# Chunk 10's gate and value weights: the low half made by an adding transfer from GpSimd's queue

## The chip, the cores and the metric

The program runs on one core of a Trainium2 chip. The metric is the device time of one execution in microseconds (us). The engines are TensorE (PE, with its weight loads shown apart as PEld), VectorE (DVE), ScalarE (ACT), GpSimd (POOL) and SyncE (SP), which issues the kernel's transfers.

## The reference, cut to what matters

Attention with a window of 16 and block summaries gives x, 3072 tokens by 512. A gated feed-forward layer follows:

```
def _moe_ref(x, w_gate, w_val, w_out):
    g = x @ w_gate                        # 512 -> 1536
    silu = g * (1.0 / (1.0 + np.exp(-g)))
    val = x @ w_val                       # 512 -> 1536
    return (silu * val @ w_out).astype(np.float32)
```

The weights come as 64-bit floats, and the answer must be exact enough that one reduced-precision product of TensorE does not do.

## The kernel before, in words

The feed-forward width of 1536 is cut into twelve chunks of 128, and the tokens into six blocks of 512. For each block and chunk TensorE computes `gate(k,j)` (12 matmuls of 128x512), `val(k,j)` (12 more) and later `down(k,j)` (12 more, into four accumulators). Twelve, because each of the four 128-row pieces of the contraction takes three products: every operand is split into a high part, rounded to TensorE's fast 32-bit format (fp32r), and a low part, the rest. The order of the three in a gate is `(wl, xh)`, `(wh, xl)`, `(wh, xh)`, so the first matmul of a gate reads the low half of the weights.

The weights are read once, while the first block (k = 0) and the second block's attention are computed. Each chunk's weights go through these steps, which the kernel names in a list written out by hand (`PROLOGUE`): `w_load` (SP, the raw 64-bit words), `w_abs` (ACT), `w_c1`, `w_c2`, `w_s1`, `w_s2` (DVE, which put the 32-bit float together bit by bit into the tile `m`), `w_hi` (a rounding copy of `m` into the high half, `=a` on ACT) and `w_lo` (`m` minus the high half into the low half, `=d` on DVE or `=p` on POOL). `gv` stands for gate and value together (128x1024), `o` for the output weights (128x512). Both halves of a chunk lie in one tile, `w_gv10` for chunk 10.

Every engine executes its instructions in the order of that list. Around the place of the change DVE does `w_lo(10,gv)`, then `w_c1(8,o)`, `w_c2(9,o)` and the key maxima of `keys(1,3)` (line 336), which overwrite a buffer that POOL's copy `kw` of the same step reads first. POOL does `w_lo(6,o)` and then the two `kw` copies of `keys(1,3)`. TensorE does `gate(0,8) val(0,8) down(0,6) tr0(1,2)`, a small transpose `pv` and then `gate(0,10)`, the first reader of `w_gv10`. After `room(1)` the memory of the tiles `m` of the chunks up to 10 is given to chunk 11's weights: SP loads `raw_v`, `raw_g` and `raw_o` of chunk 11 there.

Of the kernel before, what the change touches and what calls it, by code (L numbers as in the profile page):

```python
# [10 lines left out]
F32 = mybir.dt.float32  # L11
F32R = mybir.dt.float32r
I32 = mybir.dt.int32
AF = mybir.ActivationFunctionType
ALU = mybir.AluOpType
# [3 lines left out]
DM = H * D  # L19
DFF = 1536  # L20
BLK, WIN = 32, 16
P = 128
# [110 lines left out]
exp0(1,2) w_lo(8,gv)=d exp1(1,2) down(0,5) ah(0,7)=d w_c1(9,o) w_s2(7,o) w_c1(6,o) w_hi(7,o)=a al(0,7)=d  # L133
split(1,1)=a w_lo(9,gv)=p w_lo(7,o)=d w_c2(10,gv) w_c2(6,o) ah(0,6)=a w_abs(8,o) w_s1(10,gv) gate(0,9) w_s1(6,o)
val(0,9) down(0,7) w_s2(10,gv) silu(0,9) al(0,6)=d w_s2(6,o) gate(0,8) rcp(1,2) w_hi(6,o)=a mul(0,9) w_lo(6,o)=p
pool_values(1,2) w_hi(10,gv)=a load(1,3) w_lo(10,gv)=d w_c1(8,o) silu(0,8) w_c2(9,o) val(0,8) nrm(1,2)=a
keys(1,3) w_abs(10,o) down(0,6) tr0(1,2) load_values(1,2) rest(1,1) room(1) w_load(11,v) ah(0,9)=a w_s1(9,o)
w_c2(8,o) w_s1(8,o) mul(0,8) w_s2(8,o) values(1,2)=a w_load(11,g) pt0(1,2)=d w_s2(9,o) w_hi(8,o)=a gate(0,10)
ah(0,8)=a w_hi(9,o)=a tr1(1,2) w_lo(9,o)=p w_lo(8,o)=d al(0,9)=d pt1(1,2)=a w_load(11,o) silu(0,10) scores(1,3)
w_abs(11,v) out(1,2) w_abs(11,g) down(0,9) ttr0(1,3) ttr1(1,3) exp0(1,3) w_c1(11,g) al(0,8)=p load_values(1,3)  # L140
w_c1(11,v) w_c2(11,g) w_c1(10,o) w_s1(11,g) w_c2(10,o) w_s2(11,g) w_c2(11,v) exp1(1,3) w_hi(11,g)=a w_s1(10,o)
w_s1(11,v) val(0,10) w_s2(11,v) rcp(1,3) w_s2(10,o) w_lo(11,g)=d down(0,8) gate(0,11) mul(0,10) w_hi(10,o)=a
w_abs(11,o) nrm(1,3)=a tr0(1,3) pool_values(1,3) w_c1(11,o) w_c2(11,o) w_hi(11,v)=d w_lo(11,v)=d split(1,2)=d
w_lo(10,o)=d silu(0,11) w_s1(11,o) val(0,11) ah(0,10)=d rest(1,2) al(0,10)=d tr1(1,3) pt0(1,3)=a mul(0,11)
w_s2(11,o) values(1,3)=a w_hi(11,o)=d down(0,10) pt1(1,3)=d ah(0,11)=a al(0,11)=d out(1,3) split(1,3)=a
w_lo(11,o)=p rest(1,3) down(0,11) load(2,0)
"""


# [8 lines left out]
def body(ctx, tc, qP, kP, vT, vP, kq, kF, qF, vE, vR, vO, wgv, wends, wo, cst_in, bias_in, out):  # L158
    nc = tc.nc
# [17 lines left out]
    def subtract(e, out, a, b):  # L177
        (nc.vector if e == "d" else nc.gpsimd).tensor_tensor(out=out, in0=a, in1=b.bitcast(F32), op=ALU.subtract)  # L178

    def copy(e, out, in_):  # L180
        if e == "a":
            nc.scalar.copy(out, in_)  # L182
        else:
            (nc.vector if e == "d" else nc.gpsimd).tensor_copy(out, in_)


    W = {}
    on = ""

    def w_pool(j):  # L190
        return wts[0 if j < NJ // 2 else 1 if j < NJ - 1 else 2]

    def w_lead(j, nm):
        return LEAD if (nm, j) == ("v", NJ - 1) else 0

    def w_load(j, nm):

        n = len(nm) * DM
        w = w_pool(j).tile([P, w_lead(j, nm) + 2 * n], I32, tag=f"{nm}{j}", name=f"raw_{nm}{j}")[:, w_lead(j, nm) :]
        src = wo[j] if nm == "o" else wgv[j] if nm == "gv" else wends[j > 0, "gv".index(nm)]  # L200
        nc.sync.dma_start(w, src.bitcast(I32))  # L201
        W[nm, j] = w.rearrange("p (n t) -> p n t", t=2)

    def w_abs(j, nm):
        low, high = (W[nm, j][:, :, t] for t in range(2))
        if nm != "o" and j < NJ - 1:
            m = dec.tile([P, len(nm) * DM], F32, tag="m", name=f"m_{nm}{j}")
        else:
            m = mlp.tile([P, DM], F32, tag="o", bufs=3, name=f"m_{nm}{j}")
        nc.scalar.activation(out=m, in_=high.bitcast(F32), func=AF.Abs)  # L210
        W[nm, j] = low, high, m
# [19 lines left out]
    def w_rest(j, nm):  # L231
# [3 lines left out]
            out=f, in0=low, scalar=29, in1=f, op0=ALU.logical_shift_right, op1=ALU.bitwise_or  # L235
        )

    def w_hi(j, nm):
        m = W[nm, j][2]
        n = w_lead(j, nm) + 2 * len(nm) * DM  # L240
        w = w_pool(j).tile([P, n], F32R, tag=f"{nm}{j}", name=f"w_{nm}{j}")
        w = w[:, w_lead(j, nm) :].rearrange("p (t n d) -> p t n d", t=2, d=DM)
        hi, lo = (w[:, t].rearrange("p n d -> p (n d)") for t in range(2))
        copy(on or "a", hi, m)
        W[nm, j] = w, hi, lo, m

    def w_lo(j, nm):
        w, hi, lo, m = W[nm, j]
        subtract(on or "d", lo, m, hi)
        for i, x in enumerate(nm):  # L250
            W[x, j] = (w[:, 0, i], w[:, 1, i])


    KT, VT, ksum, vsum, X, U = {}, {}, {}, {}, {}, {}
# [570 lines left out]
    for n in WARM:  # L825
# [8 lines left out]
        "rcp": a_inverse, "nrm": a_scale, "tr0": lambda k, u: a_turn(k, u, 0), "tr1": lambda k, u: a_turn(k, u, 1),  # L834
        "pt0": lambda k, u: a_turned(k, u, 0), "pt1": lambda k, u: a_turned(k, u, 1),
        "out": a_out, "outp": a_out_pooled, "split": a_split, "rest": a_rest, "w_load": w_load, "w_abs": w_abs, "w_c1": w_range,
        "w_c2": w_shift, "w_s1": w_top, "w_s2": w_rest, "w_hi": w_hi, "w_lo": w_lo, "gate": m_up_gate,
        "silu": m_silu, "val": m_up_val, "mul": m_mul, "ah": m_high, "al": m_low, "down": m_down,
        "values": a_values, "load_values": a_load_values, "keys": a_keys, "pool_values": a_pool_values,
        "exp": a_exp, "norm": a_norm,  # L840
# [6 lines left out]
    on = ""  # L847
# [101 lines left out]
```

## Time and profile before

| what | value |
|---|---|
| timed runs, median (lowest to highest) | 674.22 us (673.66 to 674.47) |
| profiled execution, span from first to last instruction | 672.2 us |
| PE busy | 665.8 us, 99% of the span |
| DVE, ACT, POOL busy | 340.3, 292.8 and 140.9 us |
| transfers from SP's queue | 59.39 MB |

The profile lists no time of its own for the profiled execution beside its span. The median of the timed runs is 2.0 us above that span, so a span is turned into a time by adding 2.0 us. Times inside the trace count from the start of the span.

### The profile page before, as it was taken

Reading aid. Unit: us, or ns where it says so; the run is one execution under the profiler, and the core shown is the slowest. Engines: PE = TensorE matmul, PEld = TensorE weight load, DVE = VectorE, ACT = ScalarE, POOL = GpSimd, SP = SyncE. Lnnn points to the kernel's source line nnn. Section 1 sums busy time; section 2 is a strip of 40 time slices with the busy share of each in tenths; the row PEclk is TensorE's granted clock in tenths of the full one; section 3 lists DMA queues with packets and bytes.
Section 4 is the critical chain, followed back from the end, with each engine's and each line's share of the span. In section 5 each row is a group of like instructions: output and inputs, shape, how many; then the busy total and the mean of one; then the engine's idle time right before and its main releaser. Section 6 shows DMA issues by size and latency. Waiting matters only on the chain.

```text
span 672.2 us, 12396 instructions
## 1 busy us (share of the span) xinstructions
PE 665.8 (99%) x4934; PEld 543.9 (81%) x4934; DVE 340.3 (51%) x956; ACT 292.8 (44%) x723; POOL 140.9 (21%) x137
## 2 busy tenths in 40 slices
PE   8999999999999999999999999999999999999998
PEld 6688888887888888888888888888888888888886
DVE  6999999946524526446347356363352451100002
ACT  6969897834441433424415424235254151211112
POOL 4110211123221212212112122122222221111110
PEclk9999999999999999999999999999999999999999
DMA  8979743144220223403405213012122000100001
GB/s 332 393 241 359 263 141 106 61 126 129 57 57 1 57 49 119 104 5 77 105 0 168 59 47 81 23 34 71 49 57 58 0 25 0 63 1 0 1 0 64
DMA packets 72059, 60.18 MB, mean 90 GB/s; under 512 B 42273, under 2 KB 60065, under 8 KB 70465
## 3 DMA queue, kind: packets, MB, share of 16 engines
q1 hardware_dynamic: 72000, 59.39, 28.8%
q8 instruction: 39, 0.64, 0.4%
q14 instruction: 20, 0.16, 0.1%
HBM read 53.08 MB, written 6.29 MB: 88 GB/s over the span
## 4 chain that ended last, share of the span: by engine, by line
PE 96%; DMA 2%; SPq 1%; issue 0%; ACT 0%; DVE 0%; ACTq 0%
PE g L650 30%; PE v L650 29%; PE acc L697 29%; PE xo L615 4%; DMA vrows<-in_vE 2%; PE sc L447 2%; PE pp L566 1%; PE sc L458 1%; PE xo L623 1%; PE pv L415 0%; PE end L697 0%; SPq L201 0%; SPq L290 0%; SPq L285 0%; SPq L797 0%
## 5 line engine op out<-in xcount | busy, mean ns | idle before, releaser
L697 PE MATMUL acc<-w_o,ah 128*128 128x512 f32 x572 | 176.2, 389 | 0.0
L650 PE MATMUL g<-xh,w_gv 128*128 128x512 f32 x480 | 159.3, 393 | 0.0
L650 PE MATMUL v<-xh,w_gv 128*128 128x512 f32 x480 | 158.0, 390 | 0.2 <-ACT a L656 0.2
L661 DVE TENSOR_TENSOR a<-v,a 128x512 f32<-128x512 f32 x72 | 49.6, 689 | 199.8 <-PE v L650 198.1
L178 POOL TENSOR_TENSOR al<-a,ah 128x512 fp32r<-128x512 f32 x61 | 78.6, 1288 | 312.6 <-ACT ah L182 312.6
L697 PEld LDWEIGHTS acc<-w_o,ah 128*128 128x128 f32 x572 | 107.4, 188 | 22.2
L182 ACT CAST ah<-a 128x512 fp32r<-128x512 f32 x70 | 43.4, 620 | 163.3 <-DVE a L661 163.2
L697 PE MATMUL acc<-w_o,al 128*128 128x512 f32 x286 | 111.7, 391 | 0.0
L650 PEld LDWEIGHTS g<-xh,w_gv 128*128 128x128 f32 x480 | 90.1, 188 | 20.3 <-POOL w_gv L178 0.2
L650 PEld LDWEIGHTS v<-xh,w_gv 128*128 128x128 f32 x480 | 90.1, 188 | 19.2 <-ACT a L656 0.5
L656 ACT ACTIVATE a<-g 128x512 f32<-128x512 f32 x72 | 43.0, 598 | 139.6 <-PE g L650 137.8
L596 DVE STREAM_TRANSPOSE pt_short<-p_short 32x256 f32<-32x256 f32 x192 | 83.7, 436 | 19.7 <-POOL p_short L551 16.9
L650 PE MATMUL g<-xl,w_gv 128*128 128x512 f32 x240 | 93.5, 390 | 0.0
L650 PE MATMUL v<-xl,w_gv 128*128 128x512 f32 x240 | 93.4, 389 | 0.0
L697 PEld LDWEIGHTS acc<-w_o,al 128*128 128x128 f32 x286 | 53.7, 188 | 11.4 <-DVE al L178 0.2
L650 PEld LDWEIGHTS v<-xl,w_gv 128*128 128x128 f32 x240 | 45.1, 188 | 9.2
L650 PEld LDWEIGHTS g<-xl,w_gv 128*128 128x128 f32 x240 | 45.1, 188 | 8.9
L178 DVE TENSOR_TENSOR xl<-xo,xh 128x512 fp32r<-128x512 f32 x24 | 16.4, 689 | 58.3 <-ACT xh L182 58.3
L524 ACT ACTIVATE p_short<-p_short,nm 128x88 f32<-128x88 f32 x128 | 45.3, 355 | 0.2
L551 POOL TENSOR_TENSOR p_short<-p_short,ri 128x704 f32<-128x704 f32 x16 | 25.9, 1621 | 53.9 <-DVE ri L542 49.6
L650 PE MATMUL g<-xh,w_g 128*128 128x512 f32 x96 | 32.1, 396 | 0.0
L650 PE MATMUL v<-xh,w_v 128*128 128x512 f32 x96 | 31.6, 390 | 0.0
(125 smaller groups left out, 699.6 us busy)
## 6 DMA issues: line engine op xcount, KB each, us to landing
raw_gv<-in_wgv SPq DMA_DIRECT2D x10, 1024.0 KB, 11.5
raw_o<-in_wo SPq DMA_DIRECT2D x12, 512.0 KB, 12.3
out<-o SPq DMA_DIRECT2D x23, 256.0 KB, 2.1
kt<-in_kP SPq DMA_DIRECT2D x12, 384.0 KB, 4.4
vt<-in_vT SPq DMA_DIRECT2D x12, 384.0 KB, 4.1
vw<-in_vP SPq DMA_DIRECT2D x12, 384.0 KB, 3.8
kw<-in_kP SPq DMA_DIRECT2D x12, 272.0 KB, 4.9
vw<-in_vP SPq DMA_DIRECT2D x16, 192.0 KB, 3.8
```

Source lines behind the costliest of these rows:

```text
L178: (nc.vector if e == "d" else nc.gpsimd).tensor_tensor(out=out, in0=a, in1=b.bitcast(F32), op=ALU.subtract)
L182: nc.scalar.copy(out, in_)
L447: nc.tensor.matmul(sc[h][s * SQ : (s + 1) * SQ, c * SC : (c + 1) * SC], t["q"][hs, i * SQ : (i + 1) * SQ], keys[hs], start=True, stop=True,)
L458: nc.tensor.matmul(sc[h][s * QT : (s + 1) * QT, c * KC : (c + 1) * KC], t["q"][hs, qs], t["kw"][hs, i, :], start=True, stop=True,)
L524: nc.scalar.activation(out=t["p"][:, i, :kc], in_=t["p"][:, i, :kc], func=AF.Exp, scale=-1.0, bias=t["nm"][:, i : i + 1], accum_out=t["sm" ...
L551: (nc.vector if on == "d" else nc.gpsimd).tensor_tensor(out=p, in0=p, in1=ri.rearrange("p (n o) -> p n o", o=1).broadcast_to([P, 2 * NTP, ...
L596: nc.vector.transpose(out=to[r * SQ : (r + 1) * SQ, :, s * SQ : (s + 1) * SQ], in_=t["p"][s * SQ : (s + 1) * SQ, :, at : at + SQ],)
L615: nc.tensor.matmul(ps[hs, qs], vw, t["pt"][:n, h, qs], start=k not in OWN or i == 0, stop=k not in OWN)
L650: nc.tensor.matmul(ps, w[:, cs], x, start=u == 0 and n == 0, stop=u == NP - 1 and n == 2)
L656: nc.scalar.activation(out=a, in_=A.pop(("g", k, j)), func=AF.Silu)
L661: nc.vector.tensor_tensor(out=a, in0=ps, in1=a, op=ALU.mult)
L697: nc.tensor.matmul(out, a[:, ts], w[:, cs], start=begin and n == 0, stop=end and n == 2)
```

## The change

In the list one step, `w_lo(10,gv)=d`, becomes two, `w_neg(10,gv)=d w_add(10,gv)`; every other step stands where it stood. `w_neg` writes minus `m`, rounded to fp32r, into the low half, which is minus the high half; `w_add` is a transfer inside SBUF, issued from POOL's queue, that adds `m` onto it.

```
-pool_values(1,2) w_hi(10,gv)=a load(1,3) w_lo(10,gv)=d w_c1(8,o) silu(0,8) w_c2(9,o) val(0,8) nrm(1,2)=a
+pool_values(1,2) w_hi(10,gv)=a load(1,3) w_neg(10,gv)=d w_add(10,gv) w_c1(8,o) silu(0,8) w_c2(9,o) val(0,8)
...
+    def w_parts(j, nm):
+        if len(W[nm, j]) == 3:
+            m = W[nm, j][2]
+            n = w_lead(j, nm) + 2 * len(nm) * DM
+            w = w_pool(j).tile([P, n], F32R, tag=f"{nm}{j}", name=f"w_{nm}{j}")
+            w = w[:, w_lead(j, nm) :].rearrange("p (t n d) -> p t n d", t=2, d=DM)
+            hi, lo = (w[:, t].rearrange("p n d -> p (n d)") for t in range(2))
+            W[nm, j] = w, hi, lo, m
+        return W[nm, j]
...
     def w_hi(j, nm):
...
+        w, hi, lo, m = w_parts(j, nm)
         copy(on or "a", hi, m)
...
+    def w_minus(j, nm):
+        w, hi, lo, m = w_parts(j, nm)
+        if on == "d":
+            nc.vector.tensor_scalar(out=lo, in0=m, scalar1=-1.0, scalar2=None, op0=ALU.mult)
+        else:
+            nc.scalar.activation(out=lo, in_=m, func=AF.Copy, scale=-1.0)
+
+    def w_plus(j, nm):
+        w, hi, lo, m = W[nm, j]
+        nc.gpsimd.dma_start(lo.bitcast(F32), m, accum_op=ALU.add)
+        w_ready(j, nm)
...
-        "w_c2": w_shift, "w_s1": w_top, "w_s2": w_rest, "w_hi": w_hi, "w_lo": w_lo, "gate": m_up_gate,
+        "w_c2": w_shift, "w_s1": w_top, "w_s2": w_rest, "w_hi": w_hi, "w_lo": w_lo, "w_neg": w_minus, "w_add": w_plus, "gate": m_up_gate,
```

The lines of the program below the new functions stand 21 lines further down in the changed kernel (336 becomes 357, 650 becomes 671).

The first place is where the low half is made. POOL's queue there, before and then of the changed kernel (the last number of a name is a buffer's; the brackets name the semaphores that a row waits for: an engine's, a load's from SP as DMAHW, and a POOL transfer's as DMASW):

```order
L178 TENSOR_TENSOR w_gv9_1313<-m_gv9_1022,w_gv9_1313 128x1024 [waits DMAHW0_49,Activation_49]
L178 TENSOR_TENSOR w_o6_1445<-m_o6_1085,w_o6_1445 128x512 [waits DMAHW5_49,Activation_49]
L184 COPY kw_1_3_1458<-ks_3_319 128x4x24 [waits DMAHW0_49,DMAHW1_49,PE_49,Pool_49]
L184 COPY kw_1_3_1458<-ks_3_1490 128x4x24 [waits DVE_49]
L178 TENSOR_TENSOR w_o9_1556<-m_o9_1276,w_o9_1556 128x512 [waits DMAHW4_49,DMAHW2_49,Activation_49]
```

```order
L178 TENSOR_TENSOR w_gv9_1313<-m_gv9_1022,w_gv9_1313 128x1024 [waits DMAHW0_49,Activation_49]
L178 TENSOR_TENSOR w_o6_1445<-m_o6_1085,w_o6_1445 128x512 [waits DMAHW5_49,Activation_49]
L271 DMA w_gv10_1451<-m_gv10_1332 128x1024 [waits DMAHW6_49,DMAHW2_49,DVE_49]
L184 COPY kw_1_3_1458<-ks_3_319 128x4x24 [waits DMAHW0_49,DMAHW1_49,PE_49,Pool_49]
L184 COPY kw_1_3_1458<-ks_3_1491 128x4x24 [waits DVE_49]
```

The transfer stands behind `w_lo(6,o)` and ahead of both `kw` copies, and it waits for DVE. DVE's queue at the same place, before and then of the changed kernel:

```order
L356 TENSOR_REDUCE vr_1_2_1449<-vt_1_2_1169 128x24 [waits DMAHW2_49]
L178 TENSOR_TENSOR w_gv10_1451<-m_gv10_1332,w_gv10_1451 128x1024 [waits Activation_49]
L215 TENSOR_SCALAR m_o8_1382<-m_o8_1382 128x512
L219 TENSOR_SCALAR m_o9_1276<-m_o9_1276 128x512
L336 TENSOR_REDUCE ks_3_1490<-kt_1_3_1453 128x24 [waits DMAHW7_49,Pool_49]
```

```order
L377 TENSOR_REDUCE vr_1_2_1449<-vt_1_2_1169 128x24 [waits DMAHW2_49]
L265 TENSOR_SCALAR w_gv10_1451<-m_gv10_1332 128x1024
L215 TENSOR_SCALAR m_o8_1382<-m_o8_1382 128x512
L219 TENSOR_SCALAR m_o9_1276<-m_o9_1276 128x512
L357 TENSOR_REDUCE ks_3_1491<-kt_1_3_1453 128x24 [waits DMAHW7_49,Pool_49]
```

A subtraction that waited for ACT's `w_hi` became a multiplication by -1 that waits for no other engine; the key maxima keep their wait for POOL's first `kw` copy, which now stands behind the transfer.

The second place is the first reader, TensorE's `gate(0,10)`, before and then of the changed kernel:

```order
L566 MATMUL pp0_1_2_1507<-consts_104,p_1_2_1305 120x128 [waits Activation_49] x4
L394 MATMUL pv_1_2_1530<-consts_104,vr_1_2_1449 24x128 [waits DVE_49,PE_49]
L650 MATMUL g_0_10_1541<-xh_0_0_530,w_gv10_1451 128x512
L650 MATMUL g_0_10_1541<-xl_0_0_531,w_gv10_1451 128x512
L650 MATMUL g_0_10_1541<-xh_0_0_530,w_gv10_1451 128x512
```

```order
L587 MATMUL pp0_1_2_1508<-consts_104,p_1_2_1305 120x128 [waits Activation_49] x4
L415 MATMUL pv_1_2_1531<-consts_104,vr_1_2_1449 24x128 [waits DVE_49,PE_49]
L671 MATMUL g_0_10_1542<-xh_0_0_530,w_gv10_1451 128x512 [waits DMASW0_49]
L671 MATMUL g_0_10_1542<-xl_0_0_531,w_gv10_1451 128x512
L671 MATMUL g_0_10_1542<-xh_0_0_530,w_gv10_1451 128x512
```

The order is the same, and the gate's first matmul gains a wait for the transfer. SP's queue for chunk 11's loads, before and then of the changed kernel:

```order
L329 DMA vw_1_2_1512<-in_vP 96x4x128 [waits DMAHW6_49]
L201 DMA raw_v11_1520<-in_wends 128x1024 [waits DMAHW7_49,Pool_49]
L201 DMA raw_g11_1534<-in_wends 128x1024 [waits DMAHW0_49,Activation_49]
L201 DMA raw_o11_1568<-in_wo 128x1024 [waits DMAHW1_49,DVE_49]
L329 DMA vw_1_3_1642<-in_vP 96x4x128 [waits DMAHW5_49,DMAHW2_49,DMAHW6_49,PE_49,Activation_49]
```

```order
L350 DMA vw_1_2_1513<-in_vP 96x4x128 [waits DMAHW6_49]
L201 DMA raw_v11_1521<-in_wends 128x1024 [waits DMAHW7_49,Pool_49]
L201 DMA raw_g11_1535<-in_wends 128x1024 [waits DMAHW0_49,Activation_49]
L201 DMA raw_o11_1569<-in_wo 128x1024 [waits DMASW0_49,DMAHW1_49,DVE_49,Activation_49]
L350 DMA vw_1_3_1643<-in_vP 96x4x128 [waits DMAHW5_49,DMAHW2_49,DMAHW6_49,PE_49,Activation_49]
```

Only the third of these loads, `raw_o11`, gains a wait for the transfer, because it overwrites the tile `m_gv10` that the transfer reads.

## Rows read from the trace of the kernel before

**Rows 1.** Page, part 1: each engine's busy time, share, instructions.

```profile
PE 665.8 (99%) x4934; PEld 543.9 (81%) x4934; DVE 340.3 (51%) x956; ACT 292.8 (44%) x723; POOL 140.9 (21%) x137
```

**Rows 2.** Page, part 4: the chain that ended last, by engine.

```profile
PE 96%; DMA 2%; SPq 1%; issue 0%; ACT 0%; DVE 0%; ACTq 0%
```

**Rows 3.** Waits of PE: us in total, times, longest; all others are earlier loads.

```profile
PE pv L415 <- DMA vrows<-in_vE: 1.0, 1, 1.0
...
PE v L650 <- ACT a L656: 0.2, 1, 0.2
```

**Rows 4.** Timeline of DVE, 110 to 121 us: start, duration, engine, line, operation.

```profile
110.75 1.45 DVE L178 TENSOR_TENSOR w_gv<-m_gv,w_gv 128x1024 fp32r<-128x1024 f32 x1
112.12 0.48 DVE L215 TENSOR_SCALAR m_o<-m_o 128x512 f32<-128x512 f32 x1
112.52 0.41 DVE L219 TENSOR_SCALAR m_o<-m_o 128x512 int32<-128x512 int32 x1
112.86 0.94 DVE L336 TENSOR_REDUCE ks<-kt 128x24 f32<-128x768 f32 x1
...
120.92 0.28 DVE L508 CUSTOM_DVE_ANT_0 p<-sc,bias 128x120 f32<-128x120 f32 x1 [1.25 <-PE sc L458]
```

**Rows 5.** Timeline of PEld, the weight load that opens gate(0,10).

```profile
116.42 0.19 PEld L650 LDWEIGHTS g<-xh,w_gv 128*128 128x128 f32 x1
```

**Rows 6.** Tile m_gv, one group: duration ns min/median/max, first and last start.

```profile
L215 DVE TENSOR_SCALAR m_gv<-m_gv x10: 680/686/695, 20.4 to 99.3; 128x1024 f32<-128x1024 f32 x10
```

**Rows 7.** Timeline of POOL, 109 to 114 us.

```profile
109.82 1.29 POOL L178 TENSOR_TENSOR w_o<-m_o,w_o 128x512 fp32r<-128x512 f32 x1 [10.96 <-ACT w_o L182]
111.06 1.26 POOL L184 COPY kw<-ks 128x96 f32<-128x96 f32 x1
113.86 0.27 POOL L184 COPY kw<-ks 128x96 f32<-128x96 f32 x1 [1.54 <-DMA vt<-in_vT]
```

**Rows 8.** Timeline of SP, 110 to 114 us: the loads it issues.

```profile
110.86 0.34 SPq L322 DMA_DIRECT2D vt<-in_vT  x1
111.68 0.86 SPq L329 DMA_DIRECT2D vw<-in_vP  x2
112.64 0.42 SPq L201 DMA_DIRECT2D raw_v<-in_wends  x1
113.15 0.38 SPq L201 DMA_DIRECT2D raw_g<-in_wends  x1
113.63 0.38 SPq L201 DMA_DIRECT2D raw_o<-in_wo  x1
```

**Rows 9.** Transfers issued from 100 to 135 us: count, KB each, us to landing.

```profile
raw_v<-in_wends SPq DMA_DIRECT2D x1, 512.0 KB, 5.5
raw_g<-in_wends SPq DMA_DIRECT2D x1, 512.0 KB, 6.5
raw_o<-in_wo SPq DMA_DIRECT2D x1, 512.0 KB, 7.4
vt<-in_vT SPq DMA_DIRECT2D x1, 384.0 KB, 3.2
```

**Rows 10.** Windows: length, engines busy, granted PE clock, DMA share, GB/s.

```profile
108.00:112.00 4.00, 4.00 (x19) 3.30 (x19) 3.97 (x7) 2.78 (x6) 2.18 (x2) 1.00 0.05 5
112.00:114.00 2.00, 2.00 (x11) 1.65 (x10) 2.00 (x5) 2.00 (x7) 0.46 (x2) 1.00 0.88 279
114.00:116.00 2.00, 2.00 (x11) 1.60 (x10) 1.97 (x5) 1.36 (x3) 0.13 (x1) 1.00 0.95 280
116.00:118.00 2.00, 2.00 (x13) 1.73 (x12) 2.00 (x5) 1.16 (x3) 0.00 (x0) 1.00 1.01 384
```

**Rows 11.** Timeline of ACT: the first reader of chunk 11's raw_o.

```profile
129.30 0.67 ACT L210 ACTIVATE m_o<-raw_o 128x512 f32<-128x512 f32 x1
```

**Rows 12.** Page, part 6: a load of twice the size, median us to landing.

```profile
raw_gv<-in_wgv SPq DMA_DIRECT2D x10, 1024.0 KB, 11.5
```

**Rows 13.** The chain that ended last: twelve matmuls of a gate.

```profile
107.98 2.72 PE g L650 x12
```

More of the change, by code (lines that the diff above doesn't have):

```diff
@@ L135 @@
 val(0,9) down(0,7) w_s2(10,gv) silu(0,9) al(0,6)=d w_s2(6,o) gate(0,8) rcp(1,2) w_hi(6,o)=a mul(0,9) w_lo(6,o)=p
-pool_values(1,2) w_hi(10,gv)=a load(1,3) w_lo(10,gv)=d w_c1(8,o) silu(0,8) w_c2(9,o) val(0,8) nrm(1,2)=a
-keys(1,3) w_abs(10,o) down(0,6) tr0(1,2) load_values(1,2) rest(1,1) room(1) w_load(11,v) ah(0,9)=a w_s1(9,o)
-w_c2(8,o) w_s1(8,o) mul(0,8) w_s2(8,o) values(1,2)=a w_load(11,g) pt0(1,2)=d w_s2(9,o) w_hi(8,o)=a gate(0,10)
-ah(0,8)=a w_hi(9,o)=a tr1(1,2) w_lo(9,o)=p w_lo(8,o)=d al(0,9)=d pt1(1,2)=a w_load(11,o) silu(0,10) scores(1,3)
@@ L140 @@
[L140 to L144, printed above, removed]
@@ L145 @@
-w_s2(11,o) values(1,3)=a w_hi(11,o)=d down(0,10) pt1(1,3)=d ah(0,11)=a al(0,11)=d out(1,3) split(1,3)=a
-w_lo(11,o)=p rest(1,3) down(0,11) load(2,0)
+pool_values(1,2) w_hi(10,gv)=a load(1,3) w_neg(10,gv)=d w_add(10,gv) w_c1(8,o) silu(0,8) w_c2(9,o) val(0,8)
+nrm(1,2)=a keys(1,3) w_abs(10,o) down(0,6) tr0(1,2) load_values(1,2) rest(1,1) room(1) w_load(11,v) ah(0,9)=a
+w_s1(9,o) w_c2(8,o) w_s1(8,o) mul(0,8) w_s2(8,o) values(1,2)=a w_load(11,g) pt0(1,2)=d w_s2(9,o) w_hi(8,o)=a
+gate(0,10) ah(0,8)=a w_hi(9,o)=a tr1(1,2) w_lo(9,o)=p w_lo(8,o)=d al(0,9)=d pt1(1,2)=a w_load(11,o) silu(0,10)
@@ new lines @@
+scores(1,3) w_abs(11,v) out(1,2) w_abs(11,g) down(0,9) ttr0(1,3) ttr1(1,3) exp0(1,3) w_c1(11,g) al(0,8)=p
+load_values(1,3) w_c1(11,v) w_c2(11,g) w_c1(10,o) w_s1(11,g) w_c2(10,o) w_s2(11,g) w_c2(11,v) exp1(1,3)
+w_hi(11,g)=a w_s1(10,o) w_s1(11,v) val(0,10) w_s2(11,v) rcp(1,3) w_s2(10,o) w_lo(11,g)=d down(0,8) gate(0,11)
+mul(0,10) w_hi(10,o)=a w_abs(11,o) nrm(1,3)=a tr0(1,3) pool_values(1,3) w_c1(11,o) w_c2(11,o) w_hi(11,v)=d
+w_lo(11,v)=d split(1,2)=d w_lo(10,o)=d silu(0,11) w_s1(11,o) val(0,11) ah(0,10)=d rest(1,2) al(0,10)=d tr1(1,3)
@@ L147 @@
+pt0(1,3)=a mul(0,11) w_s2(11,o) values(1,3)=a w_hi(11,o)=d down(0,10) pt1(1,3)=d ah(0,11)=a al(0,11)=d out(1,3)
+split(1,3)=a w_lo(11,o)=p rest(1,3) down(0,11) load(2,0)
 """
@@ L236, in w_rest, with w_ready @@
         )
-    def w_hi(j, nm):
[L239 to L243, printed above, removed]
+    def w_parts(j, nm):
[7 more added lines that the diff above has]
+        return W[nm, j]
+    def w_ready(j, nm):
+        w = W[nm, j][0]
+        for i, x in enumerate(nm):
+            W[x, j] = (w[:, 0, i], w[:, 1, i])
+    def w_hi(j, nm):
+        w, hi, lo, m = w_parts(j, nm)
         copy(on or "a", hi, m)
-        W[nm, j] = w, hi, lo, m
     def w_lo(j, nm):
@@ L249, in w_lo @@
         subtract(on or "d", lo, m, hi)
-        for i, x in enumerate(nm):
-            W[x, j] = (w[:, 0, i], w[:, 1, i])
+        w_ready(j, nm)
[8 more added lines that the diff above has]
+        nc.gpsimd.dma_start(lo.bitcast(F32), m, accum_op=ALU.add)
+        w_ready(j, nm)
     KT, VT, ksum, vsum, X, U = {}, {}, {}, {}, {}, {}
```

## The prediction, as put on record before the result

> **What bounds the kernel now.** The page's shares come first: TensorE is busy 665.8 us, 99% of the span, and the next engine, DVE, 340.3 us [rows 1]. The chain that ended last says the same: 96% of it is PE, and DVE's share rounds to zero [rows 2]. The waits of PE then tell whether another engine ever holds it up: the longest waits lie in the opening (1.0 us for a load of the value rows), and inside the feed-forward there is one of 0.2 us [rows 3]. So the span is TensorE's own work, and an edit off TensorE can make the kernel faster only by the little that TensorE waits; it can make it slower by any amount by which it makes TensorE wait. The question is one of slack: when is the low half of chunk 10 finished, and when does TensorE want it?
>
> Before, DVE makes it from 110.75 to 112.20 us [rows 4]. The gate's first weight load, which reads it, starts at 116.42 [rows 5]. That is 4.2 us of slack, and the change spends it.
>
> **The change part by part.** *Removed:* the subtraction on DVE, 1.45 us there [rows 4]. *Added on DVE:* a multiplication by a constant of the same 128x1024. Ten such operations with one SBUF input take 686 ns [rows 6], so DVE gives back 0.76 us. TensorE has no wait that this could shorten, so I book no gain. It starts where the subtraction did, at 110.75, behind the sum over values that DVE does first, and ends at 110.75 + 0.69 = 111.44.
>
> *Added on POOL:* the transfer. POOL is free at 109.82 + 1.29 = 111.11 [rows 7], earlier than 111.44, so DVE's end releases it. The trace holds no transfer from POOL's queue and none that adds, so its price must be bounded from the transfers that SP issued around it. They are slow there because they come together: vt, two vw, raw_v, raw_g and raw_o are issued between 110.86 and 113.63 [rows 8], and the transfer engines go from a share of 0.05 before 112 to 0.88, 0.95 and 1.01 in the three windows after it [rows 10]. The 384 KB of vt, first in line, land 3.2 us after issue; the three loads of 512 KB, the size of the new transfer, land after 5.5, 6.5 and 7.4 us [rows 9]. The lower bound is vt's 3.2 us. The upper bound is the 11.5 us of loads of 1024 KB [rows 12], because an addition has to read both halves, 1024 KB, to write 512 KB. A gain is excluded: the matmul that reads the result cannot start sooner than its predecessors on PE allow. I take 7.4 us, that of raw_o: same size, in the same crowd, and the slowest of the three because the new transfer also has to read more than a load does and its issue comes on top. In its favour it is issued 1.2 us before raw_v, and raw_o no longer competes with it. Hence landing at 111.44 + 7.4 = 118.84, and a stall of TensorE of 118.84 - 116.42 = 2.42 us.
>
> POOL's issue time is also unknown. From below it is what SP needs, 0.34 to 0.42 us [rows 8]; from above the 1.26 us of the kw copy at 111.06 [rows 7], the longest thing that POOL does there. The 7.4 us contain SP's issue; up to 0.9 us more is kept for the range.
>
> *Moved, and what is queued behind the wait:* POOL's two kw copies go behind the transfer. The first, done at 112.32 before, would be done at about 111.44 + (0.4 to 1.3) + (0.3 to 1.3), so 112.1 to 114.0. DVE's key maxima wait for it; they started at 112.86 [rows 4] and could now, with DVE 0.76 us ahead, start at about 112.1, so this costs DVE up to 1.9 us and takes back its gain. DVE has the slack: it stands idle 1.25 us ahead of 120.92, waiting for TensorE's scores [rows 4], and these scores come behind gate(0,10), later by the stall. Cost zero. Without that cover the worst is 1.9 - 0.76 = 1.1 us behind the old times, still under the idle time.
>
> On SP's queue raw_o of chunk 11 waits for the landing: 118.84 instead of 113.63. With its 7.4 us it is there at 126.2; ACT reads it at 129.30 [rows 11], itself later by the stall. Cost zero; it would begin to cost if the transfer landed after 121.9 plus the stall, which moves along with it. raw_v and raw_g of chunk 11 keep their issue times, though they share the engines with the new transfer.
>
> *Sum:* the profiled span 672.2 + 2.4 = 674.6 us; with the 2.0 us by which the median lies above the span, 676.6. A stall is not won back later, because TensorE has next to no other waits to shorten.
>
> **Where a rule is weighed.** The kw copy of 128x96 takes 1.26 us at 111.06, while DVE does the subtraction, and 0.27 us at 113.86 [rows 7]: something on DVE can hold POOL up by 1.0 us. The Trainium skill, SBUF — State Buffer, section "SBUF: two separate sides", says that GpSimd writes a transfer's descriptors through a port that it shares with DVE and is shut out while DVE runs an operation that takes both ports; that speaks against a transfer from this queue while DVE is packed. The trace agrees as far as a copy goes; no row shows a descriptor. By that rule the sum would be about 677.6 instead of 676.6, and it is one of the rivals below.
>
> **The rivals.**
> 1. *The transfer is hidden* (the other side: not slower). It lands as fast as vt, after 3.2 us, at 114.64, or as raw_v, after 5.5 us, at 116.94: stall 0 to 0.5 us, so 674.2 to 674.7. For it: at 111.44 only vt and the start of vw are ahead, and the transfer engines have just come from a share of 0.05 [rows 10]. Against it: by 112.6 the crowd is there, and an addition moves more than a load. Measurement tells this kernel from no change at about 0.2%, 1.35 us, so the deciding point is a landing at 116.42 + 1.35 = 117.77, 6.3 us after DVE's end. The Trainium skill, DMA: Bandwidth & Descriptors, section "Anatomy of one DMA — SWDGE (gpsimd) path", fits a transfer on this path by 2.0 us plus bytes over 436 GB/s; an estimate by that page is 3.2 us for 512 KB, and the time would be 674.2. No run shows it in a crowd.
> 2. *The issue is late.* POOL is held up by DVE's next two operations, 0.48 and 0.41 us [rows 4], or as its copy was, by 1.0 us: landing 119.8, stall 3.4, time 677.6.
> 3. *The addition costs its double reading in full*: 11.5 us, landing 122.94, stall 6.5 us, time 680.7. raw_o would then land at 130.3, against ACT's need at 129.30 + 6.5, so nothing is added.
> 4. *The clock falls in the stall.* The granted clock is 1.00, the level of 2.4 GHz, in all windows around [rows 10]; no row shows the other level, and no pause of 2.4 us. If the gate behind the stall ran at 1.2 GHz, its twelve matmuls would take 2.72 us longer [rows 13]: 679.3. Nothing in the rows speaks for it.
> 5. *DVE's relief reaches TensorE.* The place would be the 0.2 us wait for ACT [rows 3]: 674.0 at best, from the moment that this wait proves to hang on DVE. That is below what a measurement can tell, so a gain of over 0.2% needs something that no row shows.
>
> **How the numbers follow.** The forecast, landing 6.3 to 8.4 us after DVE's end, has 0.43, with a range of its own of 675.6 to 677.6. Hidden: 0.30; late issue: 0.10; double reading or an otherwise slow transfer: 0.10; clock: 0.04; faster: 0.03. Slower by over 0.2% is 0.43 + 0.10 + 0.10 + 0.04 = 0.67, within 0.2% is 0.30, faster 0.03. The range goes from 673.8, the hidden case with the spread of the runs before, to 681.0, the double reading; it leaves out the faster case and the worst of the slow ones, less than 0.1.
>
> **What would show it.** In the changed trace DVE's multiplication should take 0.69 us and end near 111.4. POOL's transfer should appear behind it, the first kw copy 0 to 1.7 us later than before. TensorE should have one new wait, at gate(0,10), for a transfer into w_gv, of 1.4 to 3.5 us, and all later gates should be shifted by it. raw_o's issue on SP should move from 113.6 to about 119. If TensorE does not wait there, the transfer was quicker than every 512 KB load beside it; if the wait is over 5 us, the addition itself is slow. A wait elsewhere on TensorE, at gate(0,11) or down(0,9) above all, would mean that I misjudged the slack behind POOL.

## The result, and the profile after

| what | before | changed |
|---|---|---|
| timed runs, median (lowest to highest) | 673.99 us (673.66 to 674.47) | 678.92 us (677.58 to 681.11) |
| profiled execution: its own time | not listed | 678.97 us |
| profiled execution: span | 672.2 us | 677.3 us |
| mean granted clock of TensorE | 1.000 | 0.997 |

The changed kernel is slower: the ratio is 1.0073, with a 95% interval from 1.0061 to 1.0085. The time is inside the range on record, 673.8 to 681.0; it is 2.3 us above the forecast of 676.6 and outside the forecast's own range of 675.6 to 677.6. The median before has one more execution in it (673.76 us) than the table ahead of the prediction. In the profiled execution of the changed kernel the time is 1.7 us above the span.

The page's busy line, which answers to [rows 1], and the waits of PE, which answer to [rows 3]:

```profile
PE 667.5 (99%) x4934; PEld 543.9 (80%) x4934; DVE 339.9 (50%) x956; ACT 292.7 (43%) x723; POOL 141.5 (21%) x138
```

```profile
PE g L671 <- DMA w_gv<-m_gv: 2.7, 1, 2.7
```

TensorE has one large new wait, at the place that was forecast, for the transfer. The second thing to see is its own busy time: the same 4934 matmuls took 667.5 us instead of 665.8. The start of the gate and of the next one, of chunk 11, in PE's timeline before:

```profile
116.44 0.47 PE L650 MATMUL g<-xh,w_gv 128*128 128x512 f32 x1
...
130.18 0.39 PE L650 MATMUL g<-xh,w_g 128*128 128x512 f32 x1
```

The same places in the changed kernel, and then windows of 2 us of it (columns as in [rows 10], the granted clock ahead of the DMA share):

```profile
116.47 0.27 PE L415 MATMUL pv<-consts,vr 128*24 128x128 f32 x1
119.47 0.50 PE L671 MATMUL g<-xh,w_gv 128*128 128x512 f32 x1 [2.73 <-DMA w_gv<-m_gv]
119.81 0.40 PE L671 MATMUL g<-xl,w_gv 128*128 128x512 f32 x1
...
121.46 0.63 PE L671 MATMUL g<-xl,w_gv 128*128 128x512 f32 x1
...
134.84 0.39 PE L671 MATMUL g<-xh,w_g 128*128 128x512 f32 x1
```

```profile
116.00:118.00 2.00, 0.74 (x6) 0.42 (x4) 2.00 (x4) 1.08 (x3) 0.00 (x0) 1.00 0.98 186
118.00:120.00 2.00, 0.53 (x2) 0.49 (x3) 2.00 (x4) 1.55 (x3) 0.30 (x1) 1.00 1.03 402
120.00:122.00 2.00, 2.00 (x8) 1.53 (x7) 0.17 (x1) 0.00 (x0) 2.00 (x2) 0.72 0.86 250
122.00:124.00 2.00, 2.00 (x7) 1.50 (x6) 0.00 (x0) 0.00 (x0) 0.55 (x1) 0.50 0.30 117
124.00:126.00 2.00, 2.00 (x54) 1.62 (x54) 0.43 (x5) 1.43 (x3) 0.00 (x0) 0.93 0.00 0
```

The gate starts at 119.47 instead of 116.44, 3.03 us late. (PE's row counts 2.73, from the end of the matmul `pv`, which the gate's first matmul overlapped before.) At first its matmuls are as long as ever (0.40 us); from about 121 us on they take 0.63, and the granted clock is 0.72 and then 0.50, TensorE's lower level of 1.2 GHz. In this execution it fell 1.4 us after TensorE had gone back to work. The next gate, of chunk 11, starts at 134.84 where it stood at 130.18, 4.66 us late; the further 1.63 us are the low clock. The last 0.4 us of the difference of 5.1 us between the spans come at the end of the program, ahead of the last product on DVE, and no experiment was aimed at them.

What happened to the transfer itself, in the timelines of POOL and DVE (which answer to [rows 7] and [rows 4]) and in the times to landing ([rows 9]):

```profile
109.87 1.30 POOL L178 TENSOR_TENSOR w_o<-m_o,w_o 128x512 fp32r<-128x512 f32 x1 [10.94 <-ACT w_o L182]
112.04 1.00 POOL L271 DMA_DIRECT2D w_gv<-m_gv  x1 [0.87 <-DVE w_gv L265]
112.75 0.57 POOL L184 COPY kw<-ks 128x96 f32<-128x96 f32 x1
```

```profile
110.80 0.92 DVE L265 TENSOR_SCALAR w_gv<-m_gv 128x1024 fp32r<-128x1024 f32 x1
...
113.35 0.95 DVE L357 TENSOR_REDUCE ks<-kt 128x24 f32<-128x768 f32 x1 [0.97 <-POOL kw L184]
```

```profile
w_gv<-m_gv POOLq DMA_DIRECT2D x1, 512.0 KB, 7.4
raw_v<-in_wends SPq DMA_DIRECT2D x1, 512.0 KB, 7.4
raw_g<-in_wends SPq DMA_DIRECT2D x1, 512.0 KB, 8.2
raw_o<-in_wo SPq DMA_DIRECT2D x1, 512.0 KB, 5.0
```

POOL began to issue at 112.04, and the transfer landed 7.4 us later, at 119.4. Beside it raw_v and raw_g took 1.9 and 1.7 us longer to land than before. DVE waited 0.97 us for POOL's first copy, which cost nothing further on.

### The profile page after: what moved, and what is told of

The parts are those of the page before. It is cut to its first block, busy times and chain, and to the rows that moved or that the text cites. A ratio compares the mean times of both kernels' runs of the same rounds, so it can differ in the third digit from the quotient of the medians.

```text
span 677.3 us, 12402 instructions
## 1 busy us (share of the span) xinstructions
PE 667.5 (99%) x4934; PEld 543.9 (80%) x4934; DVE 339.9 (50%) x956; ACT 292.7 (43%) x723; POOL 141.5 (21%) x138
## 4 chain that ended last, share of the span: by engine, by line
PE 82%; issue 10%; ACT 3%; DMA 2%; POOL 2%; DVE 0%; SPq 0%; POOLq 0%; ACTq 0%
PE g L671 26%; PE acc L718 26%; PE v L671 25%; PE xo L636 3%; PE sc L468 2%; ACT p L545 2%; DMA w_gv<-m_gv 1%; DMA kq<-in_kF 1%; ACT pt L182 1%; POOL w_o L178 0%; POOL w_gv L178 0%; POOL kw L184 0%; ACT m_gv L210 0%; PE pp L587 0%; PE end L718 0%
```

## The experiments

Two questions were open: why the transfer needs 7.4 us, and what made the rest of the loss. Each experiment is compared with the kernel before on the same chip and in the same rounds; those medians were 674.85 us (early run, plain transfer at the same place, matmuls instead of the pause, first pause without a transfer), 674.28 (plain transfer early, less crowd, other order, cut in two) and 674.29 (second pause without a transfer, changed kernel beside it). The plain transfer early and the other order were executed once each; they are read for their traces. "First packet" below means the first packet of the transfer in the trace, counted from the start of POOL's issue.

**Earlier, in a quiet stretch.** From the changed kernel:

```
-... w_hi(10,gv)=a load(1,3) w_neg(10,gv)=d w_add(10,gv) w_c1(8,o) ...
+... w_s2(10,gv) w_neg(10,gv)=d w_add(10,gv) silu(0,9) ... w_hi(10,gv)=a load(1,3) w_c1(8,o) ...
```

> The multiplication and the adding transfer stand right behind the step that finishes m of chunk 10, 2.9 us earlier, when the transfer engines are at a share of 0.05 and only vt follows 2 us later. Crowd theory (the 7.4 us came from sharing the transfer engines with vt, vw, raw_v and raw_g): lands 3.2 to 5 us after issue, no wait of TensorE, clock 1.00, 674.0 us (673.5 to 674.6). Addition theory (7.4 us is what an adding transfer of 512 KB costs wherever it stands): lands 6.5 to 7.5 us after issue, so at about 116, wait 0 to 0.5 us, 674.0 to 674.7 us. The time is the same by both; the landing tells them apart.

675.56 us, ratio 1.0009 (1.0000 to 1.0018). TensorE has no wait for it. The time is above both forecasts (up to 674.6 and 674.7), which start from 674.0 us; the kernel before took 674.85 in these rounds, and where the 0.7 us over it come from was not looked for. The transfers' views, from 110 to 112 and from 112 to 114 us (packets, MB, share of the 16 engines), and of the landing:

```profile
q0 software_dynamic: 93, 0.38, 100.1%
```

```profile
q0 software_dynamic: 51, 0.14, 54.1%
```

```profile
w_gv<-m_gv POOLq DMA_DIRECT2D x1, 512.0 KB, 5.0
```

The adding transfer, which has queue q0 to itself, keeps all engines busy and still moves only 0.38 MB in the first 2 us. The landing of 5.0 us is at the upper end of what the crowd theory wrote; the addition costs something, and the crowd costs something.

**The same place, a plain transfer.** DVE subtracts into `m`, and the transfer only copies:

```
-nc.vector.tensor_scalar(out=lo, in0=m, scalar1=-1.0, scalar2=None, op0=ALU.mult)
+subtract("d", m, m, hi)
...
-nc.gpsimd.dma_start(lo.bitcast(F32), m, accum_op=ALU.add)
+nc.gpsimd.dma_start(lo.bitcast(F32), m)
```

> Same place, queue and size, but a plain transfer: DVE subtracts into m itself, and the transfer only copies m into the low half. Crowd theory: lands 6.5 to 7.5 us after issue as the adding one did, and as DVE's step is about 0.5 us longer, TensorE waits 2.5 to 3.5 us and the time is 677.5 to 681. Addition theory (reading both halves makes it slow): lands 4 to 5.5 us after issue, TensorE waits under 1.2 us, 674.2 to 675.5 us.

681.08 us, ratio 1.0096 (1.0081 to 1.0111), TensorE's wait 4.1 us.

```profile
112.74 0.71 POOL L271 DMA_DIRECT2D w_gv<-m_gv  x1 [1.40 <-DVE m_gv L178]
```

```profile
w_gv<-m_gv POOLq DMA_DIRECT2D x1, 512.0 KB, 8.3
```

Without an addition the landing is no sooner: the addition theory (4 to 5.5 us) falls. In the crowd, the addition is not needed to make the transfer late. The crowd theory's numbers (6.5 to 7.5 us, a wait of up to 3.5) were exceeded too. DVE's subtraction is longer than the multiplication, so this transfer was issued 0.14 us ahead of raw_v and not 0.65 us; what this later place adds to its landing was not separated.

**The plain transfer early.** The last two edits together (with `w_hi` ahead of `w_neg`, since the subtraction needs the high half).

> The plain transfer again, but early, right behind the step that finishes m (and behind ACT's rounding copy, so about 2 us later than the adding one of the early run). It completes the square adding or plain, early or in the crowd. The packets of the adding transfer kept all 16 transfer engines busy for about 3.0 us, those of the plain one for 1.3 us. If the early landing of 5.0 us was mostly that work, the plain one lands after 3.0 to 3.9 us; if it was mostly a fixed delay, after 4.5 to 5 us. No wait of TensorE for it, 673.5 to 675.5 us.

```profile
q0 software_dynamic: 144, 0.52, 65.7%
```

```profile
w_gv<-m_gv POOLq DMA_DIRECT2D x1, 512.0 KB, 3.0
```

It lands after 3.0 us. The first line is the whole transfer in a window of 2 us: 65.7% of 16 engines for 2 us is 21 engine-us. The adding one of the early run took 49 (100.1% of the first 2 us, and 54.1% of the next 2). So an addition costs 2.3 times the engines' work, and in a quiet stretch it landed 2.0 us later. The time, 679.87 us, missed for a reason of the edit's own: the rounding copy, moved ahead in ACT's queue, waited for `m`, so that silu(0,9) was late and TensorE waited 2.9 us for ACT from 108 us on:

```profile
PE g L671 <- ACT a L677: 2.9, 1, 2.9
```

```profile
112.00:114.00 2.00, 2.00 (x7) 1.55 (x6) 2.00 (x4) 0.15 (x1) 1.68 (x2) 0.57 0.58 234
```

Its clock was 0.57 in the window from 112 to 114, with no transfer to wait for.

**Less crowd.** The changed kernel, with `room(1) w_load(11,v) w_load(11,g)` put ahead of `load(1,3)`, so that these two loads are issued at 99.4 and 101.7 us.

> The changed kernel, its adding transfer at the same place, but chunk 11's raw_v and raw_g are loaded some 12 us earlier, into a quiet stretch, so that of the crowd only vt and the two vw are left. If raw_v and raw_g are what the transfer shares with: lands 5 to 6 us after issue, TensorE waits 0.2 to 1.3 us, clock 1.00, 1.0 to 2.0 us over the kernel before. If vt and vw, which are ahead of it, hold it up: lands after 6.8 to 8 us again, wait 2 to 3.5 us, 3.5 to 5 us over the kernel before.

676.05 us, ratio 1.0025 (1.0016 to 1.0035).

```profile
w_gv<-m_gv POOLq DMA_DIRECT2D x1, 512.0 KB, 5.9
```

```profile
PE g L671 <- DMA w_gv<-m_gv: 1.2, 1, 1.2
```

The first theory's numbers hold. raw_v and raw_g are worth 1.5 us of the 7.4 (2.4 and 2.5 of the 8.3 and 8.4 that the transfer took on other occasions, below). The clock stayed at 1.00, and most of the loss of 1.8 us is the wait.

**The same crowd in another order.** The two loads vw behind raw_v and raw_g instead of ahead of them:

```
-load_values(1,2) rest(1,1) room(1) w_load(11,v) ... w_load(11,g)
+rest(1,1) room(1) w_load(11,v) w_load(11,g) load_values(1,2)
```

> The changed kernel with the two vw of 192 KB, which are many short rows, moved behind raw_v and raw_g in SP's queue. If the short rows ahead of it are what holds the transfer's first packets back (they came 2.2 us after POOL's issue began, against 1.2 us in the early run): first packets within 1.5 us, landing after 5 to 6.3 us. If bytes in flight are what counts: landing after 7 to 8.5 us. TensorE may wait elsewhere for vw, so the time tells nothing.

```profile
w_gv<-m_gv POOLq DMA_DIRECT2D x1, 512.0 KB, 10.2
```

```profile
PE g L671 <- DMA w_gv<-m_gv: 5.5, 1, 5.5
```

The theory of the short rows falls: with raw_v and raw_g issued ahead of the two vw the transfer lands after 10.2 us, later than ever (681.93 us). The other theory's 7 to 8.5 us were exceeded as well. The first packet came after 4.9 us; it was 2.2 in the changed kernel and 1.6, not the 1.2 written above, in the early run. What is in flight before it holds it up; that this is a matter of bytes alone is not shown.

**Cut in two, the gate's half first.**

```
+for i in range(len(nm)):
+    half = slice(i * DM, (i + 1) * DM)
+    nc.gpsimd.dma_start(lo[:, half].bitcast(F32), m[:, half], accum_op=ALU.add)
```

> The adding transfer cut into two of 256 KB, the gate's half first; the gate waits for that half alone, the value matmuls 8 us later for the other. If the bytes in the crowd set the landing, the first half lands after 4.5 to 6 us, TensorE waits 0.2 to 1.5 us, its clock stays at 1.00, and the time is 0.7 to 2.2 us over the kernel before. If the delay ahead of the first packet sets it, the first half lands after 6.5 to 8 us and the time is 3 to 5 us over the kernel before.

678.50 us, ratio 1.0060 (1.0040 to 1.0080).

```profile
DMA to landing us min/median/max: 7.7/8.7/9.6
```

```profile
PE g L673 <- DMA w_gv<-m_gv: 3.0, 1, 3.0
```

The gate starts at 120.04, when the first half has landed, 7.7 us after its issue at 112.31. Half the bytes did not land sooner than the whole 512 KB (7.4 us, a wait of 2.7). The delay is not set by the transfer's own size. Nor is it the time to the first packet alone, 2.2 us as before: in the windows of 1 us from 117 to 120 the queue of the halves has 24.4, 8.0 and 16.6% of the 16 engines, while the loads have 82 to 88%.

**Matmuls instead of the pause.** The changed kernel, with twelve matmuls of chunk 8's weights ahead of the gate, whose sums the gate overwrites:

```
+if (k, j, nm) == (0, 10, "g"):
+    for n in range(12):
+        nc.tensor.matmul(ps, W["v", 8][0][:, :P], X[0, 0][0], start=True, stop=True)
```

> The changed kernel with 12 more matmuls, about 2.7 us, of weights that are long there, ahead of the gate that waits; their sums are thrown away. Stall-then-clock theory (2.7 us of waiting, and then about 1.7 us because TensorE's clock fell to 1.2 GHz after the pause): wait 0 to 0.4 us, granted clock 1.00 from 116 to 126 us, 676.6 us (676.3 to 677.2), so 2 us faster than the changed kernel although it does more. Rival (the low clock and the rest come from the transfer or from the crowd, not from the pause): clock 0.5 somewhere from 119 to 125 us again, 678.4 to 680 us.

678.11 us, ratio 1.0053 (1.0038 to 1.0067), so 3.3 us over the kernel before.

```profile
PE g L674 <- DMA w_gv<-m_gv: 0.9, 1, 0.9
```

```profile
120.00:122.00 2.00, 1.14 (x6) 0.68 (x5) 0.99 (x2) 0.44 (x1) 1.48 (x1) 1.00 0.74 297
122.00:124.00 2.00, 2.00 (x10) 1.63 (x9) 0.00 (x0) 0.00 (x0) 1.38 (x2) 1.00 0.72 229
```

The clock stays at 1.00 with the transfer and the crowd in place. The time is above the forecast of 676.3 to 677.2: the kernel before took 0.9 us more in these rounds, and the landing was 8.3 us on this occasion, which left 0.9 us of waiting. 2.72 us of filler [rows 13] and 0.9 are 3.6, near the 3.3 measured.

**The pause without a transfer.** The kernel before, DVE's `w_lo(10,gv)` moved behind `pt0(1,2)` and `w_s2(9,o)` (with `room(1)` and the two loads that need it), in the second run also behind `w_lo(8,o)`.

> The kernel before, with no new transfer at all; DVE's subtraction for chunk 10 is only moved behind four later steps of DVE, so that the low half is done at about 119.1 us instead of 112.2. Stall-then-clock theory: TensorE waits 2.2 to 3.0 us at the same gate, its clock falls to 1.2 GHz for a stretch behind it, and the time is 677.5 to 679.5 us, as with the transfer. Rival (the transfer itself adds something, by its queue, by its traffic or by POOL): only the wait shows, 676.2 to 677.2 us.

> No transfer: DVE's subtraction for chunk 10 stands one step later than in the late run, behind the output weights of chunk 8, so the low half is done at about 119.8 us and TensorE waits 2.8 to 3.4 us. If a pause of TensorE alone makes its clock fall, windows behind it show 0.5 to 0.8, and the time is 4.3 to 5.3 us over the kernel before, as with the transfer. If the fall needs the transfer, the clock stays at 1.00 and the time is 2.8 to 3.6 us over it.

The waits of PE of the first, with a window, and then of the second:

```profile
PE g L650 <- DVE w_gv L178: 2.4, 1, 2.4
```

```profile
120.00:122.00 2.00, 2.00 (x12) 1.63 (x11) 1.16 (x1) 0.00 (x0) 2.00 (x2) 1.00 0.76 246
```

```profile
PE g L650 <- DVE w_gv L178: 3.6, 1, 3.6
```

```profile
120.00:122.00 2.00, 1.34 (x4) 1.10 (x5) 2.00 (x2) 0.00 (x0) 2.00 (x2) 0.75 0.22 16
122.00:124.00 2.00, 2.00 (x7) 1.51 (x6) 0.29 (x1) 0.00 (x0) 1.43 (x1) 0.50 0.61 246
```

The first took 677.81 us, ratio 1.0054 (1.0035 to 1.0073), and shows both outcomes. The profiled execution (676.98 us) waited 2.4 us and kept its clock; its mean granted clock over the whole program is 1.000, and that of the execution of 677.00 us is 0.999. The other two, of 678.63 and 679.50 us, have 0.997, which is the mean of the changed kernel's profiled execution in the table at the start. So the clock seems to have fallen in these two, but they have no profile that shows where, or how long they waited. The second run settles it: no transfer, a wait of 3.6 us, the clock down to 0.50 behind it, 679.71 us, ratio 1.0076 (1.0061 to 1.0091). From this gate's start to the next one's it is 15.33 us (120.66 to 135.99), where the kernel before has 13.74. So of the 5.4 us over the kernel before 1.6 are low clock, and 3.8 are the later start of the gate. Wait and loss are a little above what was expected.

**The changed kernel beside it.** No edit.

> The changed kernel itself again, on the chip of the pause run, to set the two side by side: landing 7 to 9 us after issue, a wait of 2.5 to 4 us at the same gate, 3.5 to 7 us over the kernel before, with the spread coming from the landing and from how much of the fall of the clock an execution takes.

680.88 us, ratio 1.0101 (1.0080 to 1.0123).

```profile
w_gv<-m_gv POOLq DMA_DIRECT2D x1, 512.0 KB, 8.4
```

```profile
PE g L671 <- DMA w_gv<-m_gv: 3.7, 1, 3.7
PE warm L765 <- DVE warm L841: 1.5, 1, 1.5
PE xo L636 <- ACT pt L182: 1.2, 2, 1.0
```

```profile
124.00:126.00 2.00, 2.00 (x8) 1.50 (x7) 0.00 (x0) 0.00 (x0) 0.00 (x0) 0.50 0.21 86
```

The wait and the low clock are those of the pause run; from gate to gate it is 15.37 us here. 1.0 us of the difference to it is another wait, at 71 us, 40 us ahead of the change, behind a raw_gv for which ACT waited 1.35 us; the profiled execution of the result above did not have it. Such arrivals, the landing (7.4, 8.3 and 8.4 us of the same transfer at the same place) and the clock go into the spread of the changed kernel's times. Its eight executions have mean granted clocks from 0.995 to 0.999: the two with 0.999 took 677.58 and 678.88 us, the three with 0.995 took 680.90 to 682.62.

## Why the prediction was right, and what was missed

*The bound and the slack.* Right: TensorE had 4.2 us, the low half came later than that, and the kernel lost what TensorE waited, and more. DVE's relief was worth nothing. The prediction and [rows 3] pass over the longest wait in the list of PE before, which is for DVE at the program's start and is 1.5 us in every run here, so that nothing hangs on it:

```profile
PE warm L744 <- DVE warm L820: 1.5, 1, 1.5
```

*The issue.* DVE's multiplication took 0.92 us instead of 0.69, beside POOL's subtraction; in the early run, with POOL idle, it took 0.695. POOL began 0.3 us after DVE was done, at 112.04 instead of 111.44. This step was 0.6 us short, and so the gate was 3.0 us late and not 2.4.

*The landing.* The term of 7.4 us, taken from raw_o, measured 7.4 us, and 8.3 and 8.4 elsewhere: that it fits to the tenth is luck. The reason given, same size and same crowd, is half of it. The square of runs shows the rest: 3.0 us plain and quiet, 5.0 adding and quiet, 8.3 plain in the crowd, 7.4 to 8.4 adding in the crowd. Own size is not what counts there (the split), and what is in flight is (less crowd, other order). The traces split the landing in two. The first packet comes 1.3 and 1.6 us after the start of the issue in the quiet stretch, 2.2 to 2.5 us in the crowd, still 2.3 with raw_v and raw_g gone, 3.1 for the plain one in its later place, and 4.9 with raw_v and raw_g ahead of the vw. From there to the landing it is 5.2 to 6.0 us in the crowd, but 3.6 with raw_v and raw_g gone, close to the 3.4 of the early adding run. So, by one profile of each run, these two loads stretch the transfer's packets, and what was issued ahead of it delays the first one. Why the addition, with 2.3 times the engines' work, costs nothing more in the crowd was not settled.

*The late issue by a shared port* (a rival at 0.10) did not show in the size that it had: POOL's issue took 1.00 us in the crowd and in the early run alike, and no more than the 0.3 us between DVE's end and its start can be a hold-up, not 1.0. It is not excluded for these: POOL began just as DVE's next operation ended (112.05), and in the early run as well (0.6 us after DVE was done, at 108.71, against 108.72). In the plain early run it began inside that operation. *The hidden transfer* (0.30) was wrong here, though it is what the early run does, moved ahead of the crowd. The Trainium skill's fit, DMA: Bandwidth & Descriptors, section "Anatomy of one DMA — SWDGE (gpsimd) path", gives 3.2 us for 512 KB as an estimate; the quiet plain transfer with 3.0 us agrees with it, the other three runs of the square do not.

*The clock.* This is the step that failed: the prediction gave it 0.04, with the words "Nothing in the rows speaks for it", and left it out of the sum. The clock did fall, to 1.2 GHz for part of the gate, and cost 1.63 us in the profiled execution, less than the 2.72 that the rival had for a whole gate. Shown: it falls behind a pause without a transfer into these weights (3.6 us), and it does not fall with the transfer when matmuls fill the pause. That no row of the kernel before held such a pause was a reason for ignorance, and the prediction took it for a reason against.

*What stood behind the wait.* POOL's first copy ended at 113.32 (forecast 112.1 to 114.0), DVE's maxima began at 113.35, raw_o was issued at 119.57 (forecast about 119), and no later wait grew from them, as forecast.

*The sum.* Between the two profiles it is 3.03 us of pause, 1.63 of clock and 0.4 at the end, 5.1 in all. Against the forecast of 676.6 that is 0.6 too little for the issue, 1.6 for the clock and 0.4 for the end; 0.3 of it came back because the forecast added 2.0 us from the span to the time, where the changed kernel has 1.7. The range held the time by its upper end, which the double reading had set; that rival did not happen.

No version beats the kernel before. The early transfer equals it within 0.2%, and with TensorE at 99% and 0.2 us of waiting inside the feed-forward [rows 3] a cheaper DVE step has next to nothing to give.

## What to carry to other kernels

Price a transfer by what is in flight when it is issued: the same 512 KB landed after 3.0 us (a copy) and 5.0 us (an addition) in a quiet stretch, and after 7.4 to 10.2 us in a burst of loads, whether it added or copied; half of it took 7.7 us there. If a consumer waits for it, move its issue ahead of the burst. A pause of TensorE in the middle of dense matmuls can cost more than its length: here 1.6 us of lower clock on top of waits of 2.7, 3.6 and 3.7 us, while behind waits of 0.9 and 1.2 us the clock stayed at 1.00. Behind a wait of 2.4 us it stayed in the one execution with a profile.

## What the runs showed of the hardware that was not expected

An adding transfer inside SBUF keeps the transfer engines busy 2.3 times as long as a plain one of the same size (49 against 21 engine-us for 512 KB), and POOL takes 1.00 us instead of 0.71 to issue it. The clock's fall came at no fixed place: 1.4 us after TensorE had gone back to work in the changed kernel, 0.3 us after it in the run with a pause of 3.6 us, and 0.3 us before it, still in the pause, in the run with the wait of 5.5 us, whose gate starts at 122.59 with the clock at 0.50 already. And twelve useless matmuls in a pause of 3 us made the kernel no slower than waiting did: 3.3 us over the kernel before, against 4.9 and 6.6 us for the changed kernel on its two occasions.
